# A decode step over a 16,384-long key and value cache: the tile becomes a pair of heads

## The chip, the core and the metric

The kernel runs on one core of a Trainium2 chip; the other seven are idle. The metric is the device time of one execution in microseconds (us), as the median of several executions. The engines are named as in the profile: PE is the matrix engine (PEld its weight loads), DVE the vector engine, ACT the scalar engine, POOL the general one, and SP the one that here does nothing but start DMAs.

## What is computed

Two layers, one token for each of two batches, model width 576. Each layer is an attention block over a cache and then a small two-norm MLP. Nearly all bytes are those of the cache: K and V are each 2 batches x 32 heads x 16,384 positions x 128, in bf16, 268 MB each, and **both layers read the same cache**.

```
q = (x @ wq).reshape(B, Sq, H, Dh).transpose(0, 2, 1, 3)          # 32 heads of 128
scores = einsum("bhqd,bhkd->bhqk", q, k_cache) * (Dh ** -0.5)
p = softmax(scores)
o = einsum("bhqk,bhkd->bhqd", p, v_cache)
return o.transpose(0, 2, 1, 3).reshape(B, Sq, H * Dh) @ wo

x = x + A(layernorm(x));  x = x + B(layernorm(x))     # layer 0
x = x + A(layernorm(x));  x = x + B(layernorm(x))     # layer 1, the same weights
```

B is a layernorm, a 576 x 576 projection with gelu, a shift over one position (which leaves zeros), w2, then layernorm, w3 (576 x 4608), gelu and w4 (4608 x 576).

## The kernel before

**Tiles.** A unit of work is one head of one batch (64 of them, `order`, L580). Its K is one DMA of 4,096 KB and its V another (`plan_tile`, L471): partition p holds 128 consecutive positions, 32 KB in one run. Six places of 32 KB a partition (`NSLOT`, `TILE`) take the tiles in turn. `tile_order` (L594) puts K of head s before V of head s - 1.

**The order on SP.** `Store.plan` (L278) lists all DMAs in advance. `pump` (L289) puts the first of the list on SP's queue when every 128-byte cell of its destination has been released, and never lets a later one pass. At run time the DMA waits for the last instruction that read those cells. Weights go through the same list: those of layer 0 through a window of about 27 KB a partition, whose addresses are written out by hand (`WINDOW`, L359), and those of layer 1 into places that are free at the end.

**One head** (loop at L1115). K has 128 blocks of 128 positions in two halves of 64. The first 32 of each half go through PE in eight chunks of eight blocks: `transposes` (L1261) into one of four PSUM buffers, `evacuate` (L1267) by ACT into SBUF, and two chunks later `scores` (L1279), matmuls with one column of q. The other 32 of each half go through DVE in four `dots` (L1306): a multiply by q, broadcast over the partitions by `q_spread` (L1208), then a sum over 128. `softmax_max` (L1327) takes the maximum on DVE and lets POOL take it over the partitions; `softmax_exp` (L1339) is two exps on ACT; `pv` (L1359) is 128 matmuls with V as weights. The maximum, exp and pv of head s - 1 stand inside head s.

**Waiting for tiles.** `landed` (L1188) puts a relay on POOL: POOL waits for the DMA and then raises a semaphore for PE and, for K, one for DVE. POOL's all-reduce stands in the same order.

**Loops.** Heads 1 to 63 of each layer are a loop of 21 turns of three heads on PE, ACT and DVE (L1134, `Graph._loop`); `HEAD` sets the place of PE's loop head in a block of instruction text. Everything else is unrolled.

**Held over.** At the end of layer 0 the last three K and two V tiles and 13,824 B a partition of a third V stay for layer 1, whose order begins with those heads. In the gaps of layer 0's weight work, `ahead` and `lay` (L691, L711) transpose the last head's K early: four chunks wait in PSUM, twelve are put back in place. Layer 1 starts with `early_scores` (L1292) on these. `last_head` (L1150) ends each layer's attention.

Of the kernel before, what the change touches and what calls it, by code (L numbers as in the profile page):

```python
# [32 lines left out]
class Graph:  # L33
# [79 lines left out]
    def column(self, ap, s):  # L113
        if self.shift is None:
            return ap[:, s:s + 1]
        return ap[:, bass.ds(self.shift + s, 1)]
# [222 lines left out]
class KB:  # L339
# [4 lines left out]
    TILE = 32768  # L344
    NSLOT = 6
    CARRY = 2
    HELD = 3
# [4 lines left out]
    PB = 32  # L352
# [11 lines left out]
    }  # L364
    PART = 13824
    REST = [(13824, 8192), (22016, 8192), (30208, 2560)]
# [3 lines left out]
    def __init__(self, nc, A_x, K, V, wq, wo, w1, w2, w3, w4, out):  # L370
# [12 lines left out]
        self.NB = S // 128  # L383
        self.BP = self.NB // 2
        assert self.BP == 64 and self.F % 128 == 0 and D == 576 and all(sum(x) == self.MT for x in self.GROUPS)
# [9 lines left out]
        ch, pb, bp = self.CH, self.PB, self.BP  # L395
        self.early = ([(h, b, 2 * pb + h * (bp - pb) + b - pb) for h in range(2) for b in range(pb, bp, ch)] +
                      [(h, b, h * pb + b) for h in range(2) for b in range(0, pb, ch)][self.HOLD:])
# [4 lines left out]
    def _alloc(self):  # L402
# [10 lines left out]
        self.qb = [sb(f"qb{i}", [128, 128], BF16) for i in range(self.NS)]  # L413
        self.p = [sb(f"p{i}", [128, self.NB], BF16) for i in range(self.NS)]
        self.s_dve = [sb(f"s_dve{i}", [128, 2 * (self.BP - self.PB)], FP32) for i in range(self.NS)]
        self.q_f = sb("q_f", [128, U + 1], BF16)
        self.q_col = sb("q_col", [128, self.NS], BF16)
        self.mx = sb("mx", [128, 5, self.NS], FP32)
        self.l1 = sb("l1", [128, U], FP32)
        self.l2 = sb("l2", [128, U], FP32)  # L420
        self.o_acc = sb("o_acc", [128, U + 1], FP32)
# [3 lines left out]
        share = self.s_dve[1][:, :].bitcast(BF16)  # L425
# [45 lines left out]
    def plan_tile(self, T, t, u, slot, cuts=None):  # L471
        b, hh = u % self.B, u // self.B
        src = T[b, hh].rearrange("(p j) d -> p (j d)", p=128)
        if cuts is None:
            self.store.plan((t, u), f"tile{slot}", self.slot(slot), self.TILE, [(lambda m: m, src)])
            return
        self.parts[t, u] = self.slot(slot), [lo for lo, n in cuts] + [0] * ((t, u) == self.partly())
        for lo, n in cuts:
            self.store.plan((t, u, lo), f"part{slot}_{lo // 4096}", self.slot(slot) + lo, n,
                            [(lambda m: m, src[:, lo // 2:(lo + n) // 2])])  # L480

    def partly(self):

        return "v", self.U - self.CARRY - 1

# [45 lines left out]
    def plan_all(self):  # L531
# [9 lines left out]
        place = [(i + 2) % 6 for i in range(len(tiles))]  # L541
        place[-1] = 4
        full = lambda k, m, at: (k, 0, m, at)
        hd, mt = self.H, self.MT
        for i, (t, u) in enumerate(tiles):
            self.plan_tile(source[t], t, u, place[i])
# [16 lines left out]
        ring = [i if i < 2 else (i + 1) % 6 for i in range(len(tiles))]  # L563
        for i, (t, u) in enumerate(tiles):
            q = self.TILE // 4
            cuts = (self.REST, [(q * j, q) for j in (0, 1, 3, 2)], [(q * j, q) for j in (0, 2, 1, 3)])[i] if i < 3 else None
            self.plan_tile(source[t], t, u, ring[i], cuts)
        assert ring[-6:] == [4, 5, 0, 1, 2, 3]
        self.plan_heads(1, [s[4], s[4] + r8, s[4] + 2 * r8, s[5], s[4] + 3 * r8])
        a = s[5] + row * self.WO_CUT  # L570
        self.plan_small("w1", 1, self.w1, a, (0, 64))
        a += row * self.KT
        self.plan_cols("w3", 1, self.w3, [full(0, mt, a), full(1, mt, a + w3r), full(2, mt, s[0]), full(3, mt, s[0] + w3r),
                                          full(4, mt, s[0] + 2 * w3r)])
        assert a + 2 * w3r <= self.size
        b = s[0] + 2 * w3r + w3r // 2
        assert b + g[0] <= s[1]
        self.plan_groups(1, [b, s[1], s[1] + g[1], s[1] + g[1] + g[2], s[1] + 3 * g[1], s[1] + 4 * g[1], s[2], s[2] + g[6]], CELL)

    def order(self, l):  # L580
        U = self.U
        return list(range(U)) if l == 0 else [U - 1, U - 3, U - 2] + list(range(U - 3))

    def runs(self, l):

        U = self.U
        return [(0, 0, U)] if l == 0 else [(0, U - 1, 1), (1, U - 3, 2), (3, 0, U - 3)]

    def held(self):

        U = self.U
        return {("k", u) for u in range(U - self.HELD, U)} | {("v", u) for u in range(U - self.CARRY, U)}

    def tile_order(self, l):  # L594
# [3 lines left out]
        for s in range(self.U + 1):  # L598
            if s < self.U and ("k", o[s]) not in have:
# [29 lines left out]
    def build(self):  # L629
# [10 lines left out]
        for t, k in ((self.x, "x"), (self.st[:, 1, :, :], "st1"), (self.st[:, 2, :, :], "st2"), (self.xb[:, :, :], "xb"),  # L640
                     (self.x1[:, :, :], "x1"), (self.hs[:, :, :], "hs"), (self.zero[:, :, :], "zero"),
                     (self.xn[:, :, :], "xn"), (self.xn2[:, :, :, :], "xn2"),
                     (self.q_f[:, :], "q_f")):
            self.pool(lambda e, t=t: e.memset(t, 0.0), writes=[k])
        def f(e):
# [45 lines left out]
    def ahead(self, l, n):  # L691
# [3 lines left out]
        for _ in range(n):  # L695
            u = self.order(1)[0]
            c = len(self.held_over)
            if c < self.HOLD:
                at = self.chunk + len(self.early) + c
                self.held_over.append((0, u, c, at))  # L700
                self.transposed(u, c * self.CH, ("t", c), at % self.NT)
                self.used(1, "k", u, c * self.CH, self.CH)
            elif self.made < len(self.early):
                h, b, col = self.early[self.made]
# [3 lines left out]
                self.laid.append((h * self.BP + b, i))  # L708
                self.transposed(u, h * self.BP + b, None, i, True)

    def lay(self, l, n):  # L711
# [3 lines left out]
        for _ in range(n):  # L715
            if not self.laid:
                return
            b0, i = self.laid.pop(0)
            nm, buf, keys = self.tile("k", self.order(1)[0], b0, self.CH)
            self.act(lambda e, buf=buf, i=i: e.activation(out=buf, in_=self.sps[i][:, :].bitcast(BF16), func=ACT.Copy),  # L720
                     reads=[("sps", i), ("qps", i)], writes=keys, to="tensor")
# [182 lines left out]
    def q_projection(self, l):  # L904
# [3 lines left out]
        if l:  # L908
            at = self.order(l)[0]
            self.dv(lambda e: e.tensor_copy(out=self.q_col[:, 0:1], in_=q[:, at:at + 1]),  # L910
                    reads=[("sps", 2)], writes=[("q_col", 0)])
        for s, u, n in self.runs(l)[l:]:
            self.dv(lambda e, s=s, u=u, n=n: e.tensor_copy(out=self.q_f[:, s:s + n], in_=q[:, u:u + n]),
                    reads=[("sps", 2)], writes=["q_f"])

# [46 lines left out]
    def heads_projection(self, l, i):  # L962
# [8 lines left out]
        self.rows_step(self.store.buf(nm), lo, hi, self.sps[1], rhs, ("oA" if a < n else "oB", ("s_dve", 1)), ("sps", 1), nm, i == 0)  # L971

    def shares(self, a, b):

        sums, D = self.sps[2], self.D
        keys = [(k, s) for k in ("l1", "l2") for s in range(a, b)]
# [9 lines left out]
    def normed(self, l, lo, hi):  # L986

        for s, u, n in self.runs(l):
            a, b = max(lo, s), min(hi, s + n)
            if a < b:  # L990
                v = u + a - s
                self.stt(self.otn[:, v:v + b - a], self.o_acc[:, a + 1:b + 1], 1.0 / self.D, self.linv[:, a:b],
                         ALU.mult, ALU.mult, ["prod"] + [("o", i) for i in range(a, b)], ["otn", ("s_dve", 1)])

    def dealt(self, a, b, ps, pk, masked, out, ok):
# [5 lines left out]
        for j in range(hg):  # L1001
# [3 lines left out]
                    reads=["every", "otn", ("s_dve", 1)], writes=[pk])  # L1005
# [457 lines left out]
```

## Time and profile before

| | |
|---|---|
| median of 3 runs | 2549.02 us (2548.71 to 2550.72) |
| profiled execution, span from first to last instruction | 2549.0 us |
| DMA, all queues | 1093.00 MB in 46,498 packets, mean 429 GB/s |
| tile transfers | 125 of V and 123 of K, 4096 KB each |
| PE, PEld, DVE, ACT busy | 60%, 56%, 74%, 44% |
| mean granted PE clock | 0.652 of full speed |

The profile is of one execution. Its parts are the busy time of each engine; 40 equal slices of the span (63.7 us each) with busy tenths and GB/s; the DMA queues, where q1 carries the data and q8 instruction text; the chain of waits that ended last; and groups of instructions by line, with shape, count, busy time, mean duration in ns and the idle time before them. A name like `POOLq L187` behind an idle time is what ended it: here the relay that reports a landed tile. The timeline has a start, a duration, an engine, a line and a count of merged instructions in each row, and at its end the idle time before them.

### The profile page before, as it was taken

The numbers are of one execution on the slowest core, as the hardware profiler recorded it, in microseconds if no ns is written. First come the engines' busy times: TensorE is split into PE (matmuls) and PEld (weight loads), VectorE is DVE, ScalarE is ACT, GpSimd is POOL, SyncE is SP. The second block draws the span as 40 slices with busy tenths as digits, with TensorE's granted clock in tenths as the row PEclk, the third lists the DMA queues.
The fourth block names the chain that finished last, engine by engine and source line by source line (L and its number), as shares of the span: only waits on it lengthen the run. The fifth ranks groups of instructions, "written<-read, shape, count | busy, mean of one in ns | idle before, by whom it ended". The sixth has DMA issues, their size and how long they took to land.

```text
span 2549.0 us, 75293 instructions
## 1 busy us (share of the span) xinstructions
PE 1523.7 (60%) x34486; PEld 1434.2 (56%) x34486; DVE 1875.6 (74%) x1920; ACT 1114.2 (44%) x1833; POOL 164.1 (6%) x161
## 2 busy tenths in 40 slices
PE   4655655655565565556677655555565556556556
PEld 4555555555555455555677655555555555555555
DVE  5877776777777777777649877777677777767773
ACT  3434443443444344344346444444444344434432
POOL 0000000000000000000000000000000000000000
PEclk8666666666666666666657666666666666666665
DMA  9999999999999999999999999999999999999999
GB/s 413 427 435 429 435 429 435 429 434 430 433 431 431 432 431 433 430 433 430 423 403 424 431 433 431 432 432 431 432 431 433 430 433 430 433 430 433 430 433 381
DMA packets 46498, 1093.00 MB, mean 429 GB/s; under 512 B 5114, under 2 KB 6780, under 8 KB 11516
## 3 DMA queue, kind: packets, MB, share of 16 engines
q1 hardware_dynamic: 46460, 1092.46, 100.0%
q8 instruction: 28, 0.46, 0.1%
q14 instruction: 10, 0.08, 0.0%
HBM read 1092.44 MB, written 0.00 MB: 429 GB/s over the span
## 4 chain that ended last, share of the span: by engine, by line
DMA 70%; DVE 20%; issue 8%; PE 1%; SPq 0%; POOLq 0%; DVEq 0%; ACT 0%
DMA mem<-in_A_k_cache_dram 64%; DVE s_dve L1319 9%; DVE prod L1315 9%; DMA mem<-in_B_w_dram 2%; DMA mem<-in_A_wo_dram 2%; DMA mem<-in_A_v_cache_dram 1%; DVE mx L1324 0%; SPq L98 0%; DVE mx L1332 0%; DMA mem<-in_A_wq_dram 0%; DVE q_col L1201 0%; DVE o_acc L1356 0%; DVE mx L1330 0%; PE tps L1255 0%; PE sps L882 0%
## 5 line engine op out<-in xcount | busy, mean ns | idle before, releaser
L1270 ACT ACTIVATE mem<-tps 128x1024 bf16<-128x1024 bf16 x1020 | 958.3, 1036 | 1296.0 <-PE tps L1255 1289.9
L1255 PE MATMUL tps<-ident,mem 128*128 128x128 bf16 x8160 | 813.3, 271 | 708.6 <-POOLq L187 708.1
L1319 DVE TENSOR_REDUCE s_dve<-prod 128x16 f32<-128x2048 bf16 x508 | 1161.3, 2286 | 17.4
L1255 PEld LDWEIGHTS tps<-ident,mem 128*128 128x128 bf16 x8160 | 669.2, 124 | 718.6 <-POOLq L187 717.7
L1315 DVE TENSOR_TENSOR prod<-mem,qb 128x2048 bf16<-128x2048 bf16 x508 | 620.9, 1222 | 537.1 <-POOLq L187 530.5
L1375 PE MATMUL mps<-p,mem 128*128 128x1 bf16 x16384 | 450.6, 165 | 84.5 <-POOLq L187 74.6
L1375 PEld LDWEIGHTS mps<-p,mem 128*128 128x128 bf16 x16384 | 443.1, 102 | 99.8 <-ACT p L1349 98.7
L1285 PE MATMUL sps<-q_col,mem 128*128 128x1 bf16 x8160 | 369.2, 166 | 159.1 <-ACT mem L1270 142.9
L1285 PEld LDWEIGHTS sps<-q_col,mem 128*128 128x128 bf16 x8160 | 320.7, 101 | 216.4 <-ACT mem L1270 211.8
L1335 POOL PARTITION_ALL_REDUCE mx<-mx x128 | 160.2, 1251 | 2332.4 <-DVE mx L1332 2332.4
L1345 ACT ACTIVATE p<-s_dve,mx 128x64 bf16<-128x64 f32 x128 | 44.5, 348 | 15.5
L1214 ACT ACTIVATE qb<-sps 128x128 bf16<-128x128 f32 x129 | 34.0, 263 | 24.3 <-PE sps L1211 24.3
L1211 PE MATMUL sps<-ident,q_col 128*128 128x128 bf16 x129 | 29.7, 230 | 15.6 <-DVE q_col L1201 15.6
L1349 ACT ACTIVATE p<-sps,mx 128x64 bf16<-128x64 f32 x128 | 37.5, 293 | 0.0
L1343 ACT ACTIVATE mx<-mx 128x1 f32<-128x1 f32 x128 | 30.6, 239 | 12.3 <-POOL mx L1335 12.3
L1324 DVE TENSOR_REDUCE mx<-s_dve 128x1 f32<-128x64 f32 x128 | 28.2, 220 | 4.5
L882 PE MATMUL sps<-xn,mem 128*128 128x2 bf16 x544 | 21.3, 173 | 13.6 <-DMA mem<-in_A_wq_dram 7.3
L882 PEld LDWEIGHTS sps<-xn,mem 128*128 128x128 bf16 x544 | 20.0, 119 | 14.9 <-DMA mem<-in_A_wq_dram 8.1
L1330 DVE TENSOR_REDUCE mx<-sps 128x1 f32<-128x64 f32 x128 | 27.4, 214 | 0.7 <-DVEq L259 0.7
L1356 DVE COPY o_acc<-mps 128x1 f32 (+1 forms) x130 | 19.4, 149 | 7.5 <-PE mps L1375 7.5
L1349 ACT ACTIVATION_READ_ACCUMULATOR p<-sps,mx (+1 forms) x128 | 24.2, 189 | 0.0
L1345 ACT ACTIVATION_READ_ACCUMULATOR p<-s_dve,mx (+1 forms) x128 | 23.8, 186 | 0.0
(108 smaller groups left out, 235.0 us busy)
## 6 DMA issues: line engine op xcount, KB each, us to landing
mem<-in_A_v_cache_dram SPq DMA_DIRECT2D x125, 4096.0 KB, 45.5
mem<-in_A_k_cache_dram SPq DMA_DIRECT2D x123, 4096.0 KB, 43.2
mem<-in_A_wq_dram SPq DMA_DIRECT2D x8, 1024.0 KB, 11.5
mem<-in_A_k_cache_dram SPq DMA_DIRECT2D x8, 1024.0 KB, 8.0
mem<-in_B_w_dram SPq DMA_DIRECT2D x14, 576.0 KB, 6.8
mem<-in_B_w_dram SPq DMA_DIRECT2D x7, 864.0 KB, 21.4
mem<-in_B_w_dram SPq DMA_DIRECT2D x4, 1152.0 KB, 16.6
mem<-in_A_wo_dram SPq DMA_DIRECT2D x6, 576.0 KB, 10.0
```

Of the source, the lines that this page charges most:

```text
L882: ins = pe.matmul(out[:, m * B:(m + 1) * B], lhsT=buf[:, c:c + 127 * d + 1:d], rhs=self.xn[:, k, :], start=first and m == lo, stop=False, ...
L1214: self.act(lambda e: e.activation(out=self.qb[s % self.NS][:, :], in_=qps, func=ACT.Copy), reads=[("qps", i)], writes=[("qb", s % self.NS) ...
L1255: ins = pe.transpose(out[:, j * 128:(j + 1) * 128], buf[:, j * 128:(j + 1) * 128], self.ident[:, :])
L1270: self.act(lambda e: e.activation(out=self.kt[k], in_=self.tps[t][:, :].rearrange("p (i c) -> p i c", i=self.CH), func=ACT.Copy), reads=[( ...
L1285: ins = pe.matmul(self.sps[sp][:, c * self.CH + j:c * self.CH + j + 1], lhsT=self.kt[k][:, j, :], rhs=self.q_col[:, sp:sp + 1], start=True ...
L1315: self.dv(lambda e: e.tensor_tensor(out=prod, in0=buf.rearrange("p (j d) -> p j d", d=128), in1=qbc, op=ALU.mult), reads=[("qb", s % self. ...
L1319: self.dv(lambda e: e.tensor_reduce(out=sd[:, c0:c0 + DB], in_=prod, axis=AX.X, op=ALU.add), reads=["prod"], writes=[("s_dve", s % self.NS ...
L1335: self.pool(lambda e: e.partition_all_reduce(self.mx[:, 3, m:m + 1], self.mx[:, 2, m:m + 1], channels=128, reduce_op=ROP.max), reads=[("mx ...
L1343: self.act(lambda e: e.activation(out=self.mx[:, 4, m:m + 1], in_=self.mx[:, 3, m:m + 1], func=ACT.Copy, scale=-self.scale), reads=[("mx3" ...
L1345: self.act(lambda e: e.activation(out=p[:, n:self.NB], in_=self.s_dve[s % self.NS][:, :], func=ACT.Exp, bias=self.mx[:, 4, m:m + 1], scale ...
L1349: self.act(lambda e: e.activation(out=p[:, 0:n], in_=self.sps[i][:, 0:n], func=ACT.Exp, bias=self.mx[:, 4, m:m + 1], scale=self.scale, acc ...
L1375: ins = pe.matmul(self.mps[:, 448:449], lhsT=buf[:, j * 128:(j + 1) * 128], rhs=p[:, col:col + 1], start=(h == 0 and b == 0), stop=(h == 1 ...
```

## The change

The unit becomes a pair of neighbouring heads of one batch (32 units, `W`). K of a pair is one DMA of 8,192 KB: partitions 0 to 63 hold the first head, 64 to 127 the second, 256 positions each, 64 KB in one run. There are three places instead of six. Scores and pv are matmuls with two columns, one for each head; of the scores the half of the partitions that belongs to the head is used, and p is zero in the other half. The maximum and exp are taken for each half. PE transposes 2 x 64 of a pair's 256 blocks in 16 chunks, DVE has 2 x 64 in eight dots; in the last unit of layer 0 and the first two of layer 1 it is 2 x 80 and six dots (`PB_ENDS`).

The last K of layer 0 is transposed in place while its scores are computed (`settle`), but for four chunks that wait in PSUM; its dot blocks are transposed early in the gaps as before. Held over are the last K, the last V, and 46,592 B a partition of the V before (the same number of bytes as before). Layer 1 has two units of its own ahead of the loop, and two behind. The loop body on PE is three pairs: 10 turns in layer 0, 9 in layer 1. `qb` and one `s_dve` move into spare bytes of `mem`; the accumulators, `p` and the softmax buffers become two columns wide.

The diff, cut to what is spoken of:

```
-    TILE = 32768
-    NSLOT = 6
+    TILE = 65536
+    NSLOT = 3
-    PB = 32
+    PB = 64
+    PB_ENDS = 80
+    LAST_V = [(0, 32768), (32768, 16384), (49152, 16384)]
...
     def plan_tile(self, T, t, u, slot, cuts=None):
-        src = T[b, hh].rearrange("(p j) d -> p (j d)", p=128)
+        src = T[b, 2 * j:2 * j + 2].rearrange("h (p j) d -> (h p) (j d)", p=self.HALF)
...
-        place = [(i + 2) % 6 for i in range(len(tiles))]
+        place = [2 - i % 3 for i in range(len(tiles))]
...
+        tiles[:3] = tiles[2], tiles[0], tiles[1]
+        q = self.TILE // 4
+        self.plan_tile(source["v"], *tiles[0], 0, self.REST)
+        self.plan_tile(source["k"], *tiles[1], 1, [(q * j, q) for j in range(4)])
+        for i, (t, u) in enumerate(tiles[2:]):
+            self.plan_tile(source[t], t, u, 2 - i % 3)
...
     def order(self, l):
+        return list(range(W)) if l == 0 else [W - 1, W - 2] + list(range(W - 2))
     def held(self):
+        return {("k", self.W - 1), ("v", self.W - 1)}
...
+        def unit(s, early=None):
+            stay = l == 0 and s == W - 1
...
+            def behind():
+                self.softmax_exp(l, s - 1)
+                self.landed("v", o[s - 1], False)
+                for g in range(4):
+                    self.pv(l, s - 1, o[s - 1], g)
+            self.landed("k", o[s], True)
+            if early is not None:
+                self.keep_o(s - 2)
+                self.softmax_max(l, s - 1)
+            if early == 0:
+                behind()
+            for i, c in enumerate(chunks):
+                self.transposes(l, s, o[s], c, stay)
...
+                if stay and c >= self.HOLD:
+                    self.settle(o[s], self.block(l, s, c), ...)
+                else:
+                    self.evacuate(self.chunk)
...
+                if early and i + 1 == early:
+                    behind()
...
         if l == 0:
...
+            unit(0)
+            lo, hi = 1, W - 1
         else:
...
+            for i, b0 in enumerate(range(self.HOLD * CH, self.NB, CH)):
+                self.early_scores(l, o[0], b0)
...
+            unit(1, 4)
+            unit(2, 0)
+            lo, hi = 3, W - 2
         first = self.g.mark()
+        for s in range(lo, hi):
+            unit(s)
+        self.g.loop(first, (hi - lo) // NS, 2 * NS, self.HEAD[l])
+        for s in range(hi, W):
+            unit(s)
...
     def softmax_max(self, l, s):
+        for i in range(2):
+            self.dv(lambda e, i=i: e.tensor_reduce(out=self.mx[i * h:(i + 1) * h, m, 1:2],
+                                                   in_=self.sps[m][i * h:(i + 1) * h, i:2 * n:2], axis=AX.X, op=ALU.max), ...)
...
     def pv(self, l, s, u, g):
-                ins = pe.matmul(self.mps[:, 448:449], lhsT=buf[:, j * 128:(j + 1) * 128],
-                                rhs=p[:, col:col + 1], start=(h == 0 and b == 0),
+                ins = pe.matmul(self.mps[:, 448:450], lhsT=buf[:, j * 128:(j + 1) * 128],
+                                rhs=self.p[:, col, :], start=(h == 0 and b == 0),
```

Below, K30 is the K tile of pair 30, and so on; pairs go from 0 to 31.

More of the change, by code (lines that the diff above doesn't have):

```diff
@@ L575, in plan_all @@
[L575 to L578, printed above, removed]
+        self.plan_cols("w3", 1, self.w3, [full(k, mt, a + w3r * k) for k in range(self.KT)])
+        a += w3r * (self.KT - 1) + w3r // 2
+        assert a % CELL == 0 and a + sum(g) <= self.size
+        self.plan_groups(1, [a + sum(g[:i]) for i in range(len(g))], CELL)
@@ L597, in tile_order @@
         out = []
-        for s in range(self.U + 1):
-            if s < self.U and ("k", o[s]) not in have:
+        for s in range(self.W + 1):
+            if s < self.W and ("k", o[s]) not in have:
                 out.append(("k", o[s]))
@@ L695, in ahead @@
         for _ in range(n):
[L696 to L704, printed above, removed]
+            if self.made < len(self.early):
+                b0 = self.early[self.made]
                 i = self.made % 2 if self.made else 1
@@ L1111, in attention @@
+            w, h = len(self.early) * CH, self.HALF
+            for i in range(2):
+                self.dv(lambda e, i=i: e.tensor_copy(out=self.s_dve[0][i * h:(i + 1) * h, 0:w],
+                                                     in_=self.mps[i * h:(i + 1) * h, i:2 * w:2]),
+                        reads=["mps"], writes=[("s_dve", 0)], to="vector")
+            self.first_max(l, 0)
             for x in held[1:]:
-                self.scores(*x, last=x is held[-1])
+                self.scores(*x)
```

437 lines of the change are left out of this document (247 added, 190 removed), and 8 rows, old and new, of the table WINDOW.

## The prediction

> **What bounds the kernel now.** I read the page's head and slices first, then the DMA queues by window, the chain of waits in order of time, and the timeline around one head, the start and the change of layer.
>
> ```profile
> PE 1523.7 (60%) x34486; PEld 1434.2 (56%) x34486; DVE 1875.6 (74%) x1920; ACT 1114.2 (44%) x1833; POOL 164.1 (6%) x161
> ...
> DMA  9999999999999999999999999999999999999999
> GB/s 413 427 435 429 435 429 435 429 434 430 433 431 431 432 431 433 430 433 430 423 403 424 431 433 431 432 432 431 432 431 433 430 433 430 433 430 433 430 433 381
> ```
> ```profile
> DMA 70%; DVE 20%; issue 8%; PE 1%; SPq 0%; POOLq 0%; DVEq 0%; ACT 0%
> ```
>
> No compute engine is full, but the DMA engines are in every slice. The chain's 20% of DVE is no second limit: DVE only says when a place comes free, and the transfer so released then queues for over 40 us. Two such steps, and below them the data queue from 92 to 1255 us, a window that holds the layer-0 loop:
>
> ```profile
> 130.16 43.19 DMA mem<-in_A_k_cache_dram
> ...
> 188.45 43.19 DMA mem<-in_A_k_cache_dram
> ```
> ```profile
> q1 hardware_dynamic: 17246, 502.21, 100.3%
> ```
>
> The steps are 58.29 us apart: one loop turn, six tiles of 4.19 MB, 9.715 us each, 431.7 GB/s. So time here is bytes over rate, plus stretches in which the queue runs dry, plus whatever else uses the DMA engines. The bytes do not change: 1,051 MB of K and V (two layers of 537 MB less the 22.7 MB held over, 177,664 B a partition), or 125 pair tiles of 8.39 MB at 19.43 us.
>
> **Term 1, the runs.** The timeline where the pieces of wq land, one after the next:
>
> ```profile
> 20.73 1.01 PE L882 MATMUL sps<-xn,mem 128*128 128x2 bf16 x32 [1.47 <-DMA mem<-in_A_wq_dram]
> 23.22 0.93 PEld L882 LDWEIGHTS sps<-xn,mem 128*128 128x128 bf16 x32 [1.56 <-DMA mem<-in_A_wq_dram]
> ```
>
> A piece is 1.05 MB in 8 KB runs and takes 2.49 us, so 4.19 MB take 9.95 against 9.715 in 32 KB runs. An engine then handles 32 runs instead of 8: 0.23/24, some 9 ns a run. Runs of 64 KB save each engine 8 per pair tile, 0.07 us, times 125 = 9; I take **-8 us**. Ends: nothing, if the queue cuts runs at 32 KB; -19, if tiles went throughout at the 435 GB/s of the best slices (1,051 MB over 431.7 or over 435).
>
> **Term 2, the start.** With three places instead of six, only two tiles can be in work while one fills. The steady state allows it; first the groups of the page, then a head in the timeline:
>
> ```profile
> L1319 DVE TENSOR_REDUCE s_dve<-prod 128x16 f32<-128x2048 bf16 x508 | 1161.3, 2286 | 17.4
> ...
> L1315 DVE TENSOR_TENSOR prod<-mem,qb 128x2048 bf16<-128x2048 bf16 x508 | 620.9, 1222 | 537.1 <-POOLq L187 530.5
> ```
> ```profile
> 601.02 1.22 DVE L1315 TENSOR_TENSOR prod<-mem,qb 128x2048 bf16<-128x2048 bf16 x1 [4.62 <-POOLq L187]
> ...
> 610.71 3.48 PE L1375 MATMUL mps<-p,mem 128*128 128x1 bf16 x128 [0.79 <-POOLq L187]
> ```
>
> A dot block costs DVE 3.58 us with the gap between its two instructions. A pair has eight, 28.6 us, and some 1.3 us of small operations; the last read of K comes 27.5 us after K lands, and its place is wanted 38.9 us after. That leaves 11 us. DVE idles 4.62 us before each head, 9 a pair, which covers its added maxima; exps stay at four per pair, all-reduces and SP's tile issues halve. If that cover were gone, each microsecond would count 62 times. V is read in 2 x 3.5 us, by 27 us after K lands, and its place is wanted later still.
>
> At the start DVE is late. The timeline there:
>
> ```profile
> 0.79 0.41 SPq L98 DMA_DIRECT2D mem<-in_A_k_cache_dram  x1
> ...
> 13.27 0.29 PE L662 MATMUL mps<-ident,prod 2*128 2x2 bf16 x5 [13.27 <-DMA prod<-in_A_x_dram]
> ...
> 31.61 1.23 DVE L1315 TENSOR_TENSOR prod<-mem,qb 128x2048 bf16<-128x2048 bf16 x1 [0.69 <-ACT qb L1214]
> ...
> 46.17 1.22 DVE L1315 TENSOR_TENSOR prod<-mem,qb 128x2048 bf16<-128x2048 bf16 x1
> ```
>
> x lands right behind the first tile; 13.27 - 0.79 - 9.72 leaves 2.7 us from an issue into an empty queue, beyond the transfer itself. The first tile now takes 9.7 us longer, and wq and w2 wait behind it: the first dot starts at 41.3, the second pair's 28.9 later at 70.2, and its last product ends at 97.3. Counted on in steps of 19.4, tiles land at 22.9 (K0), 56.6 (K1, behind wq and w2), 76.0 (V0) and 95.4 (K2). V1 goes into K1's place: issued at 97.4, landed at 119.5 instead of 114.8. **+5 us**, once, since DVE needs 29.9 of 38.9 us a pair and catches up. Ends 2 and 8: 3 us of DVE's small operations either way.
>
> **Term 3, the change of layer.** The window for layer-0 weights keeps its size, K31 is transposed in place with time to spare, and 12 early and 4 held chunks remain. V31 comes in three parts, so 64 matmuls, not 128, follow its landing: 1.75 us (half of 3.5) taken from a chain on which the weights partly wait. I take **-1** (0 to -1.75).
>
> **Term 4, the start of layer 1.** The timeline of before there, and two groups of the page:
>
> ```profile
> 1314.29 0.59 PE L1300 MATMUL mps<-q_col,mem 128*128 128x1 bf16 x16 [0.26 <-DVE q_f L913]
> ...
> 1319.02 0.19 PE L1300 MATMUL sps<-q_col,mem 128*128 128x1 bf16 x1 [1.64 <-issue]
> ...
> 1319.74 2.73 PE L1255 MATMUL tps<-ident,mem 128*128 128x128 bf16 x24
> ```
> ```profile
> L1270 ACT ACTIVATE mem<-tps 128x1024 bf16<-128x1024 bf16 x1020 | 958.3, 1036 | 1296.0 <-PE tps L1255 1289.9
> ...
> L1345 ACT ACTIVATE p<-s_dve,mx 128x64 bf16<-128x64 f32 x128 | 44.5, 348 | 15.5
> ```
>
> After the change SP's order is the rest of V30, K30 in quarters (into K31's place, freed by 28 chunks of scores at 0.3 us, fast enough), then K0 whole, into V31's place. V31 is read by the first pair's pv, which unit(1, 4) puts behind four chunks of transposes of K30, and these wait for all of K30. So from K30's landing (L) nothing is queued until that pv is over: first transposes done at L + 0.9 (a third of 2.73), four evacuations by L + 5.1, four exps of at most 0.35 by L + 6.5, pv of 2 x 3.5 by L + 13.5, and 2.7 into an empty queue: 16.2. Behind the same wait stand ACT's exps, POOL's all-reduce (after the relay for K30) and, on SP, K0 and all that follows. With part of a stall for code like the 1.64 at 1319.02: **+17 us** (12, if the evacuations overlap K30's last quarter after all, to 19). K0's pair then keeps DVE until some 30 us after K0 lands, K1 waits, and V1 finds K1's place about **1 us** late (0 to 3).
>
> **Term 5, the instruction text.** The instruction queue over the span, from 24 to 92, from 1255 to 1365 and from 2510 us on:
>
> ```profile
> q8 instruction: 28, 0.46, 0.1%
> ```
> ```profile
> q8 instruction: 8, 0.13, 0.8%
> ```
> ```profile
> q8 instruction: 15, 0.25, 0.9%
> ```
> ```profile
> q8 instruction: 5, 0.08, 0.8%
> ```
>
> 8, 15 and 5 are all 28: q8 runs while new code runs, and in the loops between not at all. The 28 packets of 16 KB fit PE's text. A head has 64 transposes, 64 scores, one spread and 128 pv matmuls, each a weight load and a matmul: 514 instructions. Of 2 x 34,486 instructions 4,208 lie outside the 2 x 21 turns of three heads; with each body once that is 7,292, at 63 B each. A body of 1,542 fills 6 packets, which stay. After, a pair has 1,028 and a body 3,084: 194 KB, 12 to 13 packets. Nothing in this trace shows a body of that size. Ends: it stays, and there are some 36 packets more of longer text; or it comes again in all of the 10 + 9 turns, 17 x 13 more: 257 in all. I take the second: the nearest row shows half of it kept, and by 92 us only 8 packets had come for start and loop together, so the fetch does not run far ahead. [...]
>
> Price: 0.8% of 16 engines over 68 us is 8.7 us for 8 packets, 1.09 us of one engine each. The data beside them loses more; the data queue from 38 to 95 and from 95 to 1250 us:
>
> ```profile
> q1 hardware_dynamic: 834, 24.28, 99.4%
> ```
> ```profile
> q1 hardware_dynamic: 17112, 498.64, 100.3%
> ```
>
> That is 426.0 and 431.7 GB/s: 0.33 MB less in 57 us, at 27 GB/s an engine 12 us, for six such packets and two of 8 KB, or 1.7 a packet. I take 1.3, between the two. Spread over 16 engines, 257 x 1.3/16 = **+21 us** (from 2.5, 36 x 1.09/16, to 27 at 1.7). Tiles keep all engines full, so nothing hides it. PE, 60% busy, can wait.
>
> **Term 6, the tail.** V29 leaves 256 matmuls behind its landing, 3.5 us more. Then w3 arrives:
>
> ```profile
> 2523.78 1.72 PE L882 MATMUL sps<-xn,mem 128*128 128x2 bf16 x36 [0.29 <-DMA mem<-in_B_w_dram]
> ```
> ```profile
> 2532.18 1.72 PE L882 MATMUL sps<-xn,mem 128*128 128x2 bf16 x36 [1.11 <-DMA mem<-in_B_w_dram]
> ```
>
> These are the first and last of four pieces, 2.8 us apart and 1.72 each, so 3.2 of 3.5 us are regained and w4, which ends the kernel, still waits for DMA: **0**, or 3.5 if that cover were gone. The first weights go into V28's place, read 27 us after K29 lands, 12 before V29 has filled.
>
> **The sum**: 2549.0 - 8 + 5 - 1 + 17 + 1 + 21 = **2584**. The profiled span of 2549.0 is that of the median, 2549.02; nothing is converted.
>
> **The rivals.**
> - The body stays (term 5 is 2.5): 2566. For it: no loop here is fetched again; against it: twice the size.
> - The runs are cut at 32 KB, so for the queue the change does not do what it says: term 1 is nothing, 2592. For it: nothing here runs over 32 KB; against it: nothing either.
> - K0 finds its place in time (term 4 nothing), if PE gets to the first pv while K30 still lands: 2567. Against it: PE, ACT and POOL keep their order, and all stand behind K30.
> - On the other side, faster: the rate. Should long runs pay far more than 9 ns each, at every pair tile, 35 + 5 us more must be gained over 125 tiles, 0.32 us of 19.43 each beside the 0.07, which is over 440 GB/s; from there on it decides. At 441 GB/s tiles give 51 us instead of 8, and the time is 2541. The best slices, at 435, speak against it.
>
> **How the numbers follow.** Forecast 0.68, own range 2572 to 2600; body kept 0.14; cut runs 0.07; place in time 0.05; rate 0.06. The range of 2560 to 2604 leaves out the rate and the outermost ends. About 0.2%, 5 us, is what a measurement of this kernel tells from no change. Faster: 0.05, the rate less its near edge. Same: 0.04, edges of the rate, the kept body and the place. Slower: 0.91.
>
> **What would show it.** q8 with 250 to 300 packets, some 13 in each loop turn, or some 64 and none in loops. A data queue with about 16,000 packets fewer (248 tiles of 128 runs, halved), or as many if runs are cut. A turn of three pairs near 116.6 - 0.4 + 1.1 = 117.3 us against 2 x 58.29. A dip in GB/s near 100 us and a deep one at the start of layer 1, with K0's issue behind pv; a chain that passes there through transposes, exps and pv, and at the end through w4. I am wrong if the DMA rows are full there, or if q8 stays silent in the loops.

## The result, and the profile after

| | before | after |
|---|---|---|
| median (runs) | 2549.87 us (2548.71 to 2550.93, 4) | 2627.82 us (2626.89 to 2631.12, 4) |
| profiled span | 2549.0 us | 2625.2 us |
| tenth head tile, or fifth pair tile, has landed | 115.06 us | 122.48 us |
| from there to the last V of layer 0 | 1147.57 us | 1168.40 us |
| from there to the last of wq for layer 1 | 50.34 us | 50.88 us |
| from there to the last V of layer 1 | 1194.62 us | 1240.93 us |
| from there to the last weights | 38.49 us | 39.60 us |

The change makes the kernel 78 us slower: the ratio is 1.0309, with a 95% interval of 1.0295 to 1.0324. The landing times are those at which a transfer's semaphore is complete in the two traces. By stages the 76 us between the spans are 7 at the start, 21 in layer 0, 46 in layer 1 and 2 elsewhere.

The page of the kernel after: its busy line, the slices, the DMA queues, the chain and the group of pv (busy, mean ns, idle time before it and what ended most of it).

```profile
PE 1450.1 (55%) x34579; PEld 1315.1 (50%) x34579; DVE 1853.0 (71%) x1591; ACT 1127.8 (43%) x1703; POOL 83.5 (3%) x100
...
DMA  9999999999999999999989999999999999999998
GB/s 415 387 433 427 436 427 421 425 425 426 426 424 426 432 414 430 424 425 426 384 339 383 400 431 428 430 428 421 427 422 426 425 417 430 422 430 420 429 422 358
...
q1 hardware_dynamic: 28316, 1092.45, 97.6%
q8 instruction: 303, 4.96, 0.7%
...
DMA 83%; PE 9%; DVE 3%; ACT 2%; issue 2%; SPq 1%; POOLq 0%; POOL 0%; DVEq 0%
...
L1491 PE MATMUL mps<-p,mem 128*128 128x2 bf16 x16384 | 455.4, 165 | 420.7 <-issue 203.6
```

The bytes are the same and the engines are as idle as before, so the DMA engines are still the limit. But the slices inside the loops, 429 to 435 before, are now 414 to 436, uneven, and the instruction queue has 303 packets for 28. PE itself stood 204 us in pv without a releaser; that it waits for its text there is a guess at this point, and e6 and e11 below bear it out. Two windows of the DMA queues show that the packets come in the loops: the first is from 130 to 1270 us, the second from 1510 to 2583.

```profile
q8 instruction: 133, 2.18, 0.7%
...
q8 instruction: 124, 2.03, 0.8%
```

What they do to the tiles is seen in how each tile lands. A transfer's semaphore is raised 16 times in the trace, taken here as once for each of the 16 DMA engines' shares; here are the times of the 16 behind the first of them, in us, worked out from the trace of after:

```
tile at 180.53  0.00 0.08 0.14 0.20 0.37 0.39 0.57 0.65 1.56 1.68 1.70 1.77 1.80 1.86 1.97 1.99
tile at 201.42  0.00 0.08 0.13 0.19 0.34 0.36 0.56 0.63 1.55 1.68 1.68 1.75 1.79 3.35 3.50 3.51
tile at 260.99  0.00 0.06 0.15 0.18 0.33 0.40 0.56 0.64 3.11 3.22 3.23 3.29 3.33 3.38 3.53 5.06
tile at 320.57  0.00 0.13 0.16 0.17 0.33 0.39 0.57 0.64 4.64 4.76 4.76 4.82 4.87 4.89 5.06 6.59
```

Eight engines keep together; the other eight are pushed back in turn, by 1.5 us at a time. The number of packets fits: from 108 us, where the queue had just been dry, to the four landings the trace has 8, 11, 17 and 25 of them, and of the eight shares all, then three, one and one have been pushed once more. A tile is complete with its last engine, so those that run ahead gain nothing. As long as the last engine is not pushed again, a tile takes 19.35 us; once in eight packets it is (at 201.42, 260.99 and 320.57), and that tile takes 20.9. Later in the loops a push is shared out over two or three tiles, and the spread stays near 8 us (7.7 on average from 400 to 1271 us). The engines ahead then run out of work: 41 of 110 tiles were issued less than 2.6 us before the first engine was through with the tile ahead, and 2.6 us is what a transfer takes from its issue to its flow (worked out below). The last engine does not, since each tile of the loops is issued at least 8.4 us before the one ahead of it has landed. Over the 58 tiles from 122.48 to 1271.13 us the pushes make 1148.65 - 58 x 19.35 = 26.4 us, and over the 55 from 1491.15 to 2582.69 us 27.3.

The timeline where the first dry stretch begins: V1 waits for K1's place.

```profile
96.57 2.29 DVE L1430 TENSOR_REDUCE s_dve<-prod 128x16 f32<-128x2048 bf16 x1
98.89 0.29 DVE L1436 TENSOR_REDUCE mx<-s_dve 128x1 f32<-128x128 f32 x1
99.25 0.33 SPq L98 DMA_DIRECT2D mem<-in_A_v_cache_dram  x1
```

K2 had landed at 95.39; V1 is issued at 99.25 and lands at 122.48, 27.1 after K2. The timeline at the start of layer 1, where K30 landed at 1367.77:

```profile
1367.99 2.74 PE L1354 MATMUL tps<-ident,mem 128*128 128x128 bf16 x24 [16.07 <-POOLq L187]
1368.16 1.32 POOL L1449 PARTITION_ALL_REDUCE mx<-mx  x1 [93.05 <-DMA mem<-in_A_k_cache_dram]
1369.06 3.77 ACT L1373 ACTIVATE mem<-tps 128x1024 bf16<-128x1024 bf16 x4 [23.00 <-PE tps L1354]
...
1374.40 0.43 ACT L1466 ACTIVATE p<-sps,mx 64x160 bf16<-64x160 f32 x1
...
1374.93 6.98 PE L1491 MATMUL mps<-p,mem 128*128 128x2 bf16 x256 [3.13 <-ACT p L1466]
...
1383.01 0.33 SPq L98 DMA_DIRECT2D mem<-in_A_k_cache_dram  x1
```

K0 is issued 15.2 us after K30 has landed, behind the four evacuations, the exps and pv, and lands at 1406.12: 38.3 after K30, 19.0 of them dry. Two tiles behind it are late again, by 2.6 (at 1447.36) and 5.1 (at 1491.15).

### The profile page after: what moved, and what is told of

Read it like the earlier page. It is cut to its first block, busy times and chain, and to the rows that moved or that the text cites. A ratio compares the mean times of both kernels' runs of the same rounds, so it can differ in the third digit from the quotient of the medians.

```text
span 2625.2 us, 73875 instructions
## 1 busy us (share of the span) xinstructions
PE 1450.1 (55%) x34579; PEld 1315.1 (50%) x34579; DVE 1853.0 (71%) x1591; ACT 1127.8 (43%) x1703; POOL 83.5 (3%) x100
## 3 DMA queue, kind: packets, MB, share of 16 engines
q1 hardware_dynamic: 28316, 1092.45, 97.6%
## 4 chain that ended last, share of the span: by engine, by line
DMA 83%; PE 9%; DVE 3%; ACT 2%; issue 2%; SPq 1%; POOLq 0%; POOL 0%; DVEq 0%
DMA mem<-in_A_k_cache_dram 79%; PE tps L1354 6%; DMA mem<-in_B_w_dram 3%; DVE s_dve L1430 2%; SPq L98 1%; PE mps L1491 1%; DMA mem<-in_A_v_cache_dram 1%; DVE prod L1426 1%; ACT mem L1373 1%; ACT mem L749 1%; PE sps L1395 1%; DMA mem<-in_A_wq_dram 0%; PE sps L910 0%; PE sps L1002 0%; ACT p L1466 0%
## 5 line engine op out<-in xcount | busy, mean ns | idle before, releaser
L1426 DVE TENSOR_TENSOR prod<-mem 128x2048 bf16<-128x2048 bf16 x500 | 611.5, 1223 | 598.9 <-POOLq L187 584.3
L1354 PE MATMUL tps<-ident,mem 128*128 128x128 bf16 x8128 | 715.1, 245 | 542.8 <-POOLq L187 541.6
L1354 PEld LDWEIGHTS tps<-ident,mem 128*128 128x128 bf16 x8128 | 564.3, 111 | 548.5 <-POOLq L187 546.6
L1430 DVE TENSOR_REDUCE s_dve<-prod 128x16 f32<-128x2048 bf16 x334 | 763.5, 2286 | 11.5
L1491 PE MATMUL mps<-p,mem 128*128 128x2 bf16 x16384 | 455.4, 165 | 420.7 <-issue 203.6
L1395 PE MATMUL sps<-q_col,mem 128*128 128x2 bf16 x8160 | 366.3, 166 | 145.4 <-ACT mem L1373 71.0
L1430 DVE TENSOR_REDUCE mem<-prod 128x16 f32<-128x2048 bf16 x166 | 379.5, 2286 | 5.7
L1449 POOL PARTITION_ALL_REDUCE mx<-mx x64 | 78.8, 1232 | 2482.0 <-DVE mx L647 2352.0
L1466 ACT ACTIVATE p<-sps,mx 64x128 bf16<-64x128 f32 (+1 forms) x128 | 51.4, 402 | 1.6
L1460 ACT ACTIVATE p<-s_dve,mx 64x128 bf16<-64x128 f32 (+1 forms) x86 | 37.3, 434 | 5.4
L910 PE MATMUL sps<-xn,mem 128*128 128x2 bf16 x544 | 20.9, 173 | 9.8 <-DMA mem<-in_A_wq_dram 7.4
## 6 DMA issues: line engine op xcount, KB each, us to landing
mem<-in_B_w_dram SPq DMA_DIRECT2D x7, 864.0 KB, 21.2
```

Of the source, the lines that this page charges most:

```text
L910: ins = pe.matmul(out[:, m * B:(m + 1) * B], lhsT=buf[:, c:c + 127 * d + 1:d], rhs=self.xn[:, k, :], start=first and m == lo, stop=False, ...
L1354: ins = pe.transpose(out[:, j * 128:(j + 1) * 128], buf[:, j * 128:(j + 1) * 128], self.ident[:, :])
L1395: ins = pe.matmul(self.sps[sp][:, b:b + 2], lhsT=kt[:, j, :], rhs=self.q_col[:, 2 * sp:2 * sp + 2], start=True, stop=True, skip_group_chec ...
L1426: self.dv(lambda e: e.tensor_tensor(out=prod, in0=buf.rearrange("p (j d) -> p j d", d=128), in1=qbc, op=ALU.mult), reads=self.spilt(("qb", ...
L1430: self.dv(lambda e: e.tensor_reduce(out=sd[:, c0:c0 + DB], in_=prod, axis=AX.X, op=ALU.add), reads=["prod"], writes=self.spilt(("s_dve", m ...
L1449: self.pool(lambda e: e.partition_all_reduce(self.mx[:, m, 4:6], self.mx[:, m, 2:4], channels=128, reduce_op=ROP.max), reads=[("mx2", m)], ...
```

## The experiments

All times are medians beside runs of the kernel before on the same chip (2549.4 to 2550.2 us). The kernel after was not run again beside them: what is called less than after is the distance from its 2627.82. Theory 1 is that the text of the loops is fetched again in every turn and costs 54 us; the rivals are the price of the prediction (21 us) and the three places.

**e1_short_body.** Less text in the loops of the changed kernel.

```
+    HEAD = (16, 16)
...
+        step = 4 if self.thin else 1
-            for j in range(n):
+            for j in range(0, n, step):
```

> The changed kernel, but in the loops pv takes every fourth block of V (64 of 256 matmuls, so the output is not the reference's), and the loop heads stand at slot 16 of a block of text. A loop body on PE is then some 1,940 instructions instead of 3,084; all transfers, places and waits stay. Theory 1 (the loops' text is fetched in every turn, and its packets go to 8 of the 16 DMA engines, each taking about 1.5 us of data time there): the instruction queue falls from 303 packets to about 50, tiles come every 19.35 us through both loops, and the time falls by about 54 us, from 2628 to 2574. Rival A (text on 16 engines at 1.3 us, as predicted): 21 us, 2607. Rival B (three places instead of six leave the queue dry now and then, whatever the text does): no change, 2628.

Measured: 2606.85 us (2604.56 to 2607.74). That is the figure of rival A, but not for its reason: only 93 packets of 303 had gone.

```profile
q8 instruction: 210, 3.44, 0.5%
```

The body of 8 blocks was still fetched, 86 packets in ten turns. A block is here what one packet of text brings, 16 KB (the 28 of before are 0.46 MB), and how many a body lies in is an estimate: at 63 B an instruction, from 28 packets for the 7,292 instructions counted in before, a block holds some 260, and 1,940 from slot 16 on reach into the eighth. 21 us for 93 packets are 0.23 each, against 0.08 in rival A and 0.19 in theory 1. The expectation that 8 blocks would stay was wrong.

**e2_before_six_heads.** The other way round: the kernel before with a body as long as that of after.

```
+            if s == U - NS:
+                self.g.loop(first, (U - 1 - NS) // (2 * NS), 2 * NS, self.HEAD[l])
...
-        self.g.loop(first, (U - 1) // NS, NS, self.HEAD[l])
```

> The kernel before, with six heads in a loop turn instead of three: ten turns and three heads behind, and nothing else changed, so six places, 32 KB runs and each tile's transfer as before. The body on PE is about 3,084 instructions. Theory 1: some 13 packets of text in each of 20 turns, about 290 in all, 260 of them in the loops; 260/8 x 1.5 us = 49 us, so 2599 instead of 2550. Rival A (spread over 16 engines, 1.3 us each): 21 us, 2571. Rival B (the loss of the changed kernel comes from its three places): 2550.

Measured: 2607.50 us (2606.89 to 2608.00), ratio 1.0224 (1.0207 to 1.0241). The page's q8 row and the group of pv:

```profile
q8 instruction: 305, 5.00, 0.8%
...
L1376 PE MATMUL mps<-p,mem 128*128 128x1 bf16 x16384 | 453.7, 165 | 121.8 <-POOLq L187 98.0
```

With six places, 32 KB runs and no other change, 277 more packets cost 58 us, 0.21 each: more than theory 1 had, far more than rival A, and the places have no part in it. Another rival is that PE's stalls for text, and not the packets on the DMA engines, cost the time. Here pv mostly waits for the relay, which means that the tile is late, but over all its rows PE still stood 55 us without a releaser, close to the 58 lost. The other kernels tell the two apart: PE stood 229 us in after, whose loops lost 54, and 238 in e6 below, which lost 45; in e1 it was 20, and its 154 packets more than e5's cost 32 us, again 0.21 each. The loss goes with the packets and not with the stalls. With six places the queue holds more tiles, and the spread of the 16 landing times grows to 24 us on average from 900 to 1240 us, against 8 in after.

**e3_pv0_first** and **e4_first_pair_80**, one late start each.

```
-            self.landed("k", o[s], True)
+            if early != 0 or s > 1:
+                self.landed("k", o[s], True)
...
             if early == 0:
                 behind()
+                if s == 1:
+                    self.landed("k", o[s], True)
...
-            unit(1, 4)
+            unit(1, 0)
```

> The changed kernel with one thing moved: at the start of layer 1 the first pair's exps and pv stand ahead of the relay for K30 and of K30's transposes, so V31's place comes free while K30 still lands. If the 19 us between K30 and K0 in which no tile was queued come from that order, K0 lands 19.4 us after K30. K30 is then still read by PE and DVE until 22 to 26 us after its landing, and K1, which takes its place, is late by about 5 instead of 0. The time falls by 12 to 19 us, to 2609 to 2616. If K0 waits for something else, 2628.

Measured: 2616.05 us (2613.69 to 2616.48), 11.8 less, at the edge of what was expected. K0 lands 26.2 us after K30 (1368.60), not 19.4. The timeline says why:

```profile
1363.52 1.84 PE L1494 MATMUL mps<-p,mem 128*128 128x2 bf16 x64 [1.63 <-issue]
1368.81 2.74 PE L1357 MATMUL tps<-ident,mem 128*128 128x128 bf16 x24 [3.45 <-POOLq L187]
1371.35 0.40 PE L1398 MATMUL sps<-q_col,mem 128*128 128x2 bf16 x8
...
1371.78 19.22 SPq L98 DMA_DIRECT2D mem<-in_A_k_cache_dram  x2
```

pv ends at 1365.4, before K30 lands, but K0 is issued only after the first scores of K30. `_stand_in` lets SP wait on the next PE instruction that raises the common semaphore, and that one is behind K30's relay.

```
-        return self.PB_ENDS if (l, s) in ((0, self.W - 1), (1, 0), (1, 1)) else self.PB
+        return self.PB_ENDS if (l, s) in ((0, 0), (0, self.W - 1), (1, 0), (1, 1)) else self.PB
```

> The changed kernel, but PE transposes 2 x 80 blocks of the first pair of layer 0 and DVE has six dots of it instead of eight. DVE is then 7.2 us earlier at the end of K1, so V1 is issued at about 92.1 us instead of 99.25. If DVE's late start is what makes V1 late, V1 lands 19.4 to 20 us after K2 instead of 27.1, and the time falls by 7 us, to 2621. If another reader of K1 is late too, less, down to nothing.

Measured: 2622.35 us (2621.53 to 2623.64), 5.5 less. V1 is issued at 92.78 and lands 21.7 us after K2; DVE was the cause of most of it, and 2.3 of 7.7 us are left.

**e5_body_7_blocks.** As e1, with `step = 8`.

> As e1_short_body, but pv in the loops takes every eighth block of V (32 of 256 matmuls, so again not the reference's output): the body is about 1,750 instructions and lies in 7 blocks of 16 KB, where that of e1_short_body lay in 8 and still fetched about 8.7 packets a turn (86 in ten turns). If a body of 7 blocks stays, as the one of the kernel before does, the instruction queue is silent in the loops, some 50 packets are left of 303, and at the 0.209 us a packet that e2_before_six_heads paid (58 us for 277 packets) 53 us go: 2575, with a tile every 19.35 us in both loops. If 7 packets a turn still come, about 2596. If text is not what costs, 2607, as e1_short_body.

Measured: 2574.40 us (2574.16 to 2577.03), 53.4 less than after. The first row is the page's, the second that of the window from 130 to 1250 us.

```profile
q8 instruction: 56, 0.92, 0.1%
...
q8 instruction: 5, 0.08, 0.0%
```

Here a body of 7 blocks stayed, with 5 packets of text in 1,120 us. 247 packets fewer are 0.22 us each, and of the 58 tiles from 123 to 1246 us 56 come every 19.34 to 19.37 us and two after 19.5. With most of pv left out, PE is relieved as well; but in after, with all of pv, the tiles between two pushes come 19.35 us apart too, and the last engine always has a tile queued. So the three places lose nothing in the loops, and the text is all of the loss there.

**e6_before_8_blocks** and **e11_before_7_blocks.** The kernel before with 48 instructions more in a turn, and the loop heads at two slots, 239 in e6 and 128 in e11. The diff of e6:

```
-    HEAD = (200, 60)
+    HEAD = (239, 239)
...
+            for _ in range(9):
+                ins = pe.matmul(qps, lhsT=self.wide(self.q_col[:, i:i + 1]), rhs=self.ident[:, :],
+                                start=True, stop=True, skip_group_check=True)
```

> The kernel before with q_spread's matmul done nine times over in each head (the same result, 48 instructions more in a turn) and the loop heads at slot 239 of a block instead of 200 and 60, so that the body of some 1,600 instructions lies in 8 blocks of text instead of 7. Nothing else is changed: places, runs and tiles are those of before. If 8 blocks are one too many, some 8.7 packets come in each of the 42 turns, 365 in all, and at 0.19 to 0.21 us each the time is 2619 to 2626, slower than e2_before_six_heads, whose body is twice as long. If only what does not fit is fetched again, one or two packets a turn, 2558 to 2567. If 8 blocks stay, 2550.

Measured: 2594.89 us (2592.45 to 2600.84). The slowdown came, with half of the packets that were expected. The page's row, and that of the window of one loop turn, 145 to 210 us:

```profile
q8 instruction: 218, 3.57, 0.6%
...
q8 instruction: 9, 0.15, 1.0%
```

In the next turn, 210 to 268 us, there is no q8 row at all: 9 packets come in every second turn. Why here every second and in e1 every one stays open. 190 packets more than before cost 45 us, 0.24 each. The 1.5 us of a push once in eight packets make 0.19; where the rest of the 0.21 to 0.24 comes from is not shown.

> The kernel of e6_before_8_blocks with one number changed: the loop heads stand at slot 128 of a block of text instead of 239, so the same instructions lie in 7 blocks instead of 8. In e6_before_8_blocks 9 packets came in every second turn (190 more than before in all) and the time rose by 45 us, half of what was expected. If these 45 us are the fetched text, the instruction queue is back at about 28 packets and the time at 2550. If they are the eight added matmuls in each head, 2595 again.

Measured: 2551.75 us (2550.16 to 2556.31), ratio 1.0007 (0.9997 to 1.0017).

```profile
q8 instruction: 30, 0.49, 0.1%
```

The same instructions, with the loop heads 111 slots nearer to the start of a block: 43 us, all of them text. PE's 238 us without a releaser in e6 are 6 here, so those were waits for text.

**e7_both_starts.** e4, and e3 with K30 reported by quarters and the last matmul of the first pv on the common semaphore.

```
-                sig=("v", g, keys[0]), to="vector" if g == 3 else None)
+                sig=("v", g, keys[0]), to="vector" if g == 3 and (l, s) != (1, 0) else None)
...
+                    self.landed("k", o[s], True, True)
```

> The changed kernel with e4_first_pair_80, and with e3_pv0_first in a fuller form: K30's four quarters are reported one by one as they land, and the last matmul of the first pv raises the semaphore on which SP waits. In e3_pv0_first that pv was over 3.3 us ahead of K30's landing, but K0 still landed 26.2 us after K30, 6.9 more than a tile takes: the wait of SP stands on the next PE instruction of that semaphore, the first scores of K30. If that is right, K0 lands 19.4 us behind K30; and with K30 read from its first quarter on, K1 and the next two tiles are no longer late by 2.4 and 4.8. The time falls by 5.5 (e4) + 11.8 (e3) + 6.9 and by up to 7: 2597 to 2604. If K0 is still late, 2610.

Measured: 2604.71 us (2602.13 to 2604.96), 23.1 less than after. K0 is issued at 1359.89, ahead of K30's landing at 1363.17, and lands 21.2 us after it; 1.8 stay. The shares of K30 landed 2.35 us apart, so K0 was issued only 0.9 us before the first engine had done its share, and from an issue to the flow of a transfer it takes some 2.6 us (worked out below). The later tile that was 5.1 us late is still 4.1 late.

**e8_all_three.** e5 and e7 together.

> e5_body_7_blocks and e7_both_starts together (pv in the loops takes every eighth block, so not the reference's output): pairs, 64 KB runs and three places remain, while fetched text and both late starts are gone. If these three are the whole loss, the time is below that of the kernel before by the 8 to 10 us of the longer runs, 2538 to 2550. If three places cost something of their own in the loops, above 2555.

Measured: 2553.14 us (2551.07 to 2555.00), ratio 1.0011 (1.0001 to 1.0021), 3 us above what was expected. In each loop one tile took 20.85 us and the others 19.35; V1 (2.3), K0 (1.4) and two tiles behind it (1.9 and 3.7) are still late, and these 9 us are about what the longer runs gain. So text and the two starts are the loss: 78 us have become 3 or 4.

**e9_rest_repaired.** e8 with one more pair at 2 x 80 blocks.

```
-        return self.PB_ENDS if (l, s) in ((0, 0), (0, self.W - 1), (1, 0), (1, 1)) else self.PB
+        return self.PB_ENDS if (l, s) in ((0, 0), (0, self.W - 1), (1, 0), (1, 1), (1, 2)) else self.PB
```

> As e8_all_three (pv in the loops takes every eighth block, so not the reference's output), and PE has 2 x 80 blocks of the third pair of layer 1 too, DVE six dots instead of eight. In e8_all_three one tile there, V of that pair's neighbour, which takes K1's place, came 23.0 us after the tile before it instead of 19.35; the same queue of dots on DVE as at the start of layer 0 is the suspect. If so that step is 19.4 to 20 and the time falls by 3 to 3.7 us, from 2553 to 2549.5 to 2550. If PE's or ACT's share of K1 is as late, no change.

Measured: 2557.00 us (2554.83 to 2559.81), 6.8 above its runs of before, where e8 was 3.7 above its own: some 3 us slower, and the guess was wrong. That tile now takes 26.8 us instead of 23.0, since DVE got its dots out of the way and then stood still:

```profile
1382.55 0.25 DVE L1442 TENSOR_REDUCE mx<-s_dve 128x1 f32<-128x96 f32 x1
1394.10 1.23 DVE L1432 TENSOR_TENSOR prod<-mem 128x2048 bf16<-128x2048 bf16 x1 [11.29 <-ACT mem L1319]
```

It waits for q of the next pair, which `q_spread` makes on PE and ACT only behind all chunks of this one, and there are now 20 instead of 16.

**e10_runs_of_32KB.** e9 with each tile as two DMAs.

```
-            self.store.plan((t, u), f"tile{slot}", self.slot(slot), self.TILE, [(lambda m: m, src)])
+            self.store.plan((t, u), f"tile{slot}", self.slot(slot), self.TILE, [
+                (lambda m, i=i: m[:, i * 16384:(i + 1) * 16384], src[:, i * 16384:(i + 1) * 16384]) for i in range(2)])
```

> As e9_rest_repaired (the same part of pv left out), but each tile of 8.39 MB is two DMAs of 32 KB a partition instead of one of 64 KB, so the runs have the length that they have in the kernel before, at the same places and in the same order. If the length of the runs makes the 0.08 us between 19.35 and 2 x 9.715, tiles come every 19.43 us and the time is 10 us longer than that of e9_rest_repaired. If it comes from something else of the pairs, the two are within 2 us. If two DMAs have a price of their own, more than 10.

Measured: 2564.24 us (2563.84 to 2565.95), 7.2 more than e9. The data queue of e9 from 200 to 1200 us:

```profile
q1 hardware_dynamic: 7443, 433.39, 100.1%
```

and that of e10 in the same window:

```profile
q1 hardware_dynamic: 14822, 431.69, 100.3%
```

Twice the packets, 0.4% fewer bytes: 19.43 us a pair tile again. The gain of the long runs is real. e10 also has twice as many DMAs, so its time alone does not tell the two apart, but the packets in the traces do: in this window one of 64 KB takes 2.422 us on average in e9 and two of 32 KB take 2.434 in e10, and with eight such pairs on each engine that is 0.10 us a tile. The second DMA adds one packet of 4 B on each engine, 0.009 us. So nearly all of it is the runs.

No version here is faster than the kernel before; the fastest of the changed kernel with nothing left out is e7, 2604.71 us. To do better, the text of a turn would have to fit in 7 blocks of 16 KB, the most that stayed here (e5, e11), by the estimate of 63 B some 1,800 instructions, while three pairs, the period of the three places, have 3,084; e5 and e8 got there by leaving work out.

## Why the prediction was wrong

The direction was right (2584 against 2549), and the places where most of the time is lost had been named. The size was wrong: 78 us instead of 35, and above the 2600 at which the range ended. So was the way in which text costs time.

1. **The runs, -8.** Right, and its 9 ns a run are near the 12 of e9 and e10: 0.08 us on each of some 120 tiles are 10; e10 measured 7.2.
2. **The start, +5.** 7.4. V1 was issued 1.9 us later than counted, since SP waits on the maximum behind the last dot (98.89), not on the dot's product. V1 then landed 3.9 us later than its own 19.35 (122.48 - 99.25 - 19.35), where 2.7 had been counted. The 2.7 was right for 15 of the 16 engines, whose shares had landed 2.6 late; the sixteenth was 1.3 behind them, pushed by a packet of text at 108.5, which the forecast did not have there.
3. **The change of layer, -1.** +0.5; nothing was gained there.
4. **The start of layer 1, +17 and +1.** The first was 19.0, by the chain as foretold: transposes, evacuations, exps, pv, K0's issue. It is 2.8 longer than the 16.2 that were added up: pv ended 0.6 later (14.1 behind K30), SP waited 1.1 more, for the next scores as in e3, and one engine was again pushed by text, which adds 1.1 to the 2.7 counted. The second was 7.6, two late tiles instead of one. In e8, where K0 is 1.4 late, one of them is still 3.7 late; e9 shows that DVE's dots alone do not set it, and what does stays open.
5. **The text, +21. This is the step that failed:** "Spread over 16 engines, 257 x 1.3/16". The count was right, 303 packets in all and 133 in the layer-0 loop, by a choice that the trace of before could not settle. The price was wrong in both factors, the 1.3 a little and the 16 by half. In the trace of after the packets go to eight of the 16 engines, and push each back by 1.5 us; a tile is complete with its last engine, so 8 packets cost 1.5 us and not 0.65. The loops lost 53.7 us, and 0.21 to 0.24 us a packet were measured in e2, e5, e6 and e11. Dividing by 16 takes it that the engines without a packet make up for the one that has it. They do not: each has its own share of a tile, they run ahead into the tiles that are queued, by 6.6 us at the landing at 320.57, and only the last one's landing sets when a place comes free.
6. **The tail, 0.** 1.1.

The sum by these: 2549.0 - 10 + 7.4 + 0.5 + 19.0 + 7.6 + 53.7 + 1.1 = 2628, against a span of 2625.2. The sum is too long because before had such losses too: two of its tiles, at 1262.63 and 1361.46, were 1.2 and 2.3 us late. 33 of the 44 us that the forecast missed are term 5, 7 the second gap. That a span lies 1.7 us below its run's time (2625.2 and 2626.89) had been left out.

Of the rivals, the body that stays fell with q8; the cut runs fell with e10 and with q1's 28,316 packets, 18,144 fewer; K0 finding its place in time fell with the timeline; the rate fell, as tiles came at 19.35 us and not at 19.04. The signs that were named came: 13 or 14 packets a turn, a turn of 118.8 us instead of 117.3, a dip near 100 us (387 GB/s), a deep one at the start of layer 1 (339), and K0 behind pv.

How much text stays at most was not shown by before, whose body lies in 7 blocks. In the runs 7 blocks stayed (5 packets from 130 to 1250 us in e5, 30 in the whole of e11) and 8 did not (86 in ten turns in e1, 90 from 130 to 1250 us in e6). A packet fetched again cost 0.21 to 0.24 us in a kernel whose limit is the DMA engines.

## What to carry to other kernels

When a unit of work is made larger, count the instructions of one loop turn (on PE here 1,542 before and 3,084 after), and where the loop lies in blocks of text: moving the loop head by 111 slots was worth 43 us here, about six times the 7.2 us of the longer runs in e10. A price for something that uses a few of the DMA engines is taken from when the last engine of a transfer lands (1.5 us for 8 packets here), and not from bytes in a window (0.65). With fewer places, look at each start, where no reserve is built up yet (7.4 us at the first and 19.0 at the second here), and at the instruction on which a transfer really waits, which need not be the one that reads its place.

## What was not expected of the hardware

- In after, instruction text went to 8 of the 16 DMA engines, in turn, 1.5 us of data time each: of the 16 landing times of one tile, the eight that it leaves alone stay within 0.65 us, and the last stood 2.0 us behind the first after 8 packets and 6.6 after 25.
- A loop body on PE in 7 blocks of text stayed: 5 packets came from 130 to 1250 us in e5, and 30 in the whole of e11, for 28 in before. In 8 blocks it was fetched anew, with 86 packets in ten turns at some 1,940 instructions (e1), and with 9 in every second turn at some 1,600 (e6).
- With 64 KB runs, a transfer issued into an empty queue landed 3.7 to 3.9 us later than its own 19.35 (V1 and K0 of after, K0 of e3 and e5). The queue itself accounts for 2.5 to 2.6 of this, by which 14 or 15 of the 16 shares were late; the others came 1.2 to 1.4 us behind them, with one or two packets of text in the transfer. The first tile of after, with no text beside it, landed 3.0 later.
